# Attention, Fourier mixing and an MLP on one core: the order of every queue planned anew, as the best of 24 plans

## The chip, the cores and the metric

The kernel runs on one core of a Trainium2 chip. The core has a matrix engine (TensorE, PE in the profile), an elementwise engine (VectorE, DVE), an engine for activations (ScalarE, ACT), a general engine (GpSimd, POOL) and a queue engine (SyncE, SP). They run at the same time, each working through its own list of instructions in order, and wait for one another by semaphores. Transfers between DRAM and the on-chip memory run on 16 DMA engines, issued from SP, POOL and ACT. The metric is the device time of one execution in microseconds (us).

## The reference

Inputs are q, k and v of shape 4 × 8 × 768 × 64 (batch, head, position, width), eight memory keys and values for every head, and two weight matrices of 512 × 2048 and 2048 × 512. The computation has two parts:

```python
# attention: chunks of 32 queries see 8 memory keys, 16 keys to the left, the chunk, 8 to the right
scores = scale * np.matmul(q_c, k_full.transpose(0, 1, 3, 2))
a = exp(scores - max); a = a / (sum(a) + 1e-09)
out[:, :, c_start:c_end] = np.matmul(a, v_full)
# x: heads side by side, 4 x 768 x 512
X = np.fft.fft(x, axis=1)
X = np.fft.fft(X, axis=2)
u = x + np.real(X)
un = (u - mu) / np.sqrt(var + 1e-06)
ch = np.maximum(un @ w_ch1, 0.0) @ w_ch2
return (u + ch).astype(np.float32)
```

## The kernel before, in words

**Attention** is done in 16 steps, four for each batch, of two heads each. A step loads q and k (POOL, L345 and L349) and v (SP, L358 to L367, seven transfers) into rings of three and four buffers. For batches 0 to 2, PE turns q and k (L377), ACT copies q and ACT or DVE copies k (L395, L408); batch 3's are turned by transposing transfers on SP (L382, L386). PE makes the scores in two groups (L433), ACT takes the exponential (L441), PE multiplies with the values in two groups (L457, named xa and xo) and DVE normalises into the batch's x (L467, L468).

**Fourier.** The real part of the two-dimensional transform is made by matmuls with tables of sines and cosines. For batches 1 to 3: DVE folds x (L489, L496, L497, L506), ACT rounds to 16 bits (L514), DVE takes the remainder (L519), PE multiplies along the rows of the sequence in four groups of 12 matmuls, one of them with 12 more (L529), ACT rounds (L541), DVE takes the remainder (L546), PE multiplies along the columns (L699) for half of the output tiles and a last row (L580), and DVE adds to x (L705, and L587 with L589 for the mirrored half, which needs a copy of x with its rows in reverse). That copy goes through DRAM: out on POOL (L563), turned by SP (L567 and L568, x_back from x_rows), back on POOL (L572). Batch 0 is done in its own way, so that it can start early: rows in groups L669, L675 and L688, and all six column tiles on PE. DVE then takes statistics (L713, L714), and ACT centres or scales (L720, L724). PE turns batch 0's tiles (L730); SP transposes those of the others (L748).

**MLP**, for each batch in three blocks of two 128-row tiles: 8 first-layer groups (L775) with ReLU on ACT (L784), then the second layer (L793) with the addition on DVE (L800) for batches 0 and 1. For batches 2 and 3 the second layer is made of seven products of half-size blocks (L842); DVE prepares sums and differences of the ReLU's output and of the weights (L830, `e_w2t`), and adds the products (L847).

**What sets the order.** The kernel is not written in its final order. Every piece of work is recorded by `add` as a task: its engine, an estimated cost, the tasks that it comes after, the buffers that it takes and gives back (all named in `Plan(dict(qs=NS, ks=NS, va=NV, ...))`: PSUM banks are tr, sc, xa, two of acc and two of mlp), and a rank. `behind` names a task that must have been placed first on whatever engine, `late` and `lag` shift a time, `moved` is a transfer's size in estimated us. `order` then walks through estimated time and gives each idle engine the lowest-ranked task that can start. The list that it returns is the order in which instructions are emitted, so each engine's queue follows it; the planner's times have no other part in the program. PSUM banks of tasks with `pick` are chosen in that walk too.

```python
for t in plan.order():
    t["emit"]()
```

**Zero products.** While PE has no task to start between the first scores and the first low part of batch 0 (`plan.filling`, which names `t_sc[0, 0]`), the planner places matmuls with zeros (`e_fill`, L902). **The gate.** q and k of step 4 are loaded behind a copy of one element of step 3's v on POOL (`e_gate`, L956), which holds that queue until v has landed. **The weights** are loaded on POOL, the first layer's between steps 5 and 6, the second layer's after step 6 (L1062, L1067).

Of the kernel before, what the change touches and what calls it, by code (L numbers as in the profile page):

```python
# [36 lines left out]
class Plan:  # L37
# [3 lines left out]

    LAG = {"PE": 0.2}
    FIRST = 45.0
    WARM = 18.0
    SLACK = 0.7
    FILL = 0.17
    filling, fill = None, None
# [14 lines left out]
    def share(self, now):  # L62
# [26 lines left out]
        if self.seen < now:  # L89
            self.flow, self.seen = {}, now  # L90

    def order(self):
        now, idle = 0.0, {}
        self.flow, self.seen = {}, 0.0
        waiting, since = {}, {}
# [4 lines left out]
        gives = []  # L100
        placed = []
        while any(waiting.values()):
# [5 lines left out]
            for e, ts_ in waiting.items():  # L108
                if idle.get(e, 0.0) > now:
                    continue  # L110
                held = False
                for t in ts_:
# [28 lines left out]
                    cost = t["cost"] * (2.0 if e == "PE" and now < self.WARM else 1.0)  # L141
                    idle[e] = t["end"] = now + cost
                    if t["moved"]:
                        self.flow.setdefault(e, []).append([t, t["moved"], now + cost * t["head"]])
                        self.share(now)
                        t["end"] = t["done"]
                    else:
# [10 lines left out]
                else:  # L158
                    if e == "PE" and self.filling and self.filling[0]["at"] is not None \
# [5 lines left out]
                        moved = True  # L165
            if not moved:
                times = ([v for v in idle.values() if v > now] + [g[0] for g in gives]
                         + [t["done"] + x for t in placed for x in (0.0, self.SLACK, 4.0, 8.0)
                            if t["done"] + x > now])
# [8 lines left out]
def kernel(  # L178
# [709 lines left out]
    for i in range(NV):  # L888
# [4 lines left out]
                       rank=(0, 1, 2, 3)[i])  # L893
    t_masks = add("POOL", 0.6, e_masks, rank=16)
    dz = cpool.tile([P, P], BF16)
# [42 lines left out]
    t_gate, LATE, t_flip = None, 1.0, [None]  # L938
    t_uz = add("POOL", 0.4, lambda: [nc.gpsimd.memset(kU[i], 0.0) for i in range(NKU)], rank=20)

    def attention(n):
        nonlocal t_gate
        b, pr = seq[n]
        first = b == 0
# [14 lines left out]
        mk = t_mk[n] = add("ACT" if n == HP else "DVE", 0.25, lambda: e_mkT(n), [t_mkT, t_kTz[n % NKT], t_mk.get(n - 1)],  # L959
                           take=("kTb",), behind=t_norm.get((HP - 1, 1)) if n in (HP, HP + 1) else None)  # L960
        if b >= TURNED:
            eq = add("SP", 1.2, lambda: e_flip_q(n), [lq], take=("qT",), give=("qs",),
                     late=5.0, loose=True, behind=t_flip[0])
            t_flip[0] = tk = add("SP", 1.2, lambda: e_flip_k(n), [lk, t_uz], take=("kU",),
                                 give=("ks",), late=5.0, loose=True, behind=eq)
            ek = add("DVE", 0.6, lambda: e_kT(n), [tk, mk], give=("kU",), lag=4.0)
        else:
            tq = add("PE", 0.40, lambda: e_turn_q(n), [lq, t_idb], take=("tr",), give=("qs",))
# [4 lines left out]
            tk = add("PE", 0.43, lambda: e_turn_k(n), [lk, t_idb, t_kz if n == 0 else t_kzs],  # L973
                     take=(ktag,), give=("ks",))
            ek = add(dve[0], 1.25 if dve[1] else 1.04, lambda: e_kT(n, dve[1]), [tk, mk],
                     give=(ktag,))
        xs_ = []
        for g in range(2):
            s_ = add("PE", 0.32, lambda g=g: e_scores(n, g), [eq, ek], take=("sc",),
                     give=("qT", "kTb") if g == 1 else ())  # L980
            t_sc[n, g] = s_
            t_exp[n, g] = x_ = add("ACT", 1.12, lambda g=g: e_exp(n, g),
                     [s_, t_masks, t_after.get(n)], take=("e1",), give=("sc",))
            xs_.append(x_)
            if not first and g == 0:
                continue
            tag = "mlp" if first and g == 1 else "xa"
            if not first:
                vp = dict(of=("mlp", "acc"))
                pick_of["v", n] = vp  # L990
                v_ = add("PE", 1.5, lambda: [e_values(n, i) for i in range(2)],
                         xs_ + [lv, t_low[n % NV]], take=("xa",), pick=vp, give=("e1", "e1", "va"))
                for i in range(2):
# [5 lines left out]
            v_ = add("PE", 0.85, lambda g=g: e_values(n, g), [x_, lv, t_low[n % NV]], take=(tag,),  # L999
                     rank=len(plan.tasks) + (50 if (n, g) == (2, 1) else 25) if first else None,  # L1000
                     give=("e1", "va") if g == 1 else ("e1",))
# [135 lines left out]
    def fourier(b):  # L1137
# [8 lines left out]
        for par in range(2):  # L1146
# [8 lines left out]
            for ab in range(2):  # L1155
# [6 lines left out]
                         give=("fold",) if ab == 1 else ())  # L1162
                rw = add("PE", 1.95 if par == 0 and ab == 1 else 1.0,
                         lambda par=par, ab=ab: e_rows(b, par, ab), [lo, t_sines],
# [4 lines left out]
        return columns_of(b, t_rest)  # L1169

    def columns_of(b, t_rest):
        t_dn, t_un, cols = {}, {}, {}
        allr = list(t_rest.values())
        kts, sa = (0, 1, 2, 3, 4, 5), None
        thirds = set()

# [15 lines left out]
        def columns(kt):  # L1192
            if b > 0 and kt > 2:
                if kt == 3:
                    cols[kt] = add("PE", 0.7, lambda: e_last_row(b), [t_sum[0]])
                return
# [8 lines left out]
        for i, kt in enumerate(kts):  # L1205
# [13 lines left out]
            if b in EVEN:  # L1219
                if i % 2:  # L1220
                    t0, t1 = kts[i - 1], kt
                    sc_ = add("POOL", 2.6, lambda t0=t0, t1=t1: e_scale(b, t0, t1 - t0), [sa])
                    for t in (t0, t1):
                        un = add("ACT", 0.72, lambda t=t: e_un(b, t), [sc_], take=("un",))
# [4 lines left out]
            un = add("ACT", 0.72, lambda kt=kt: e_un(b, kt), [sa], take=("un",))  # L1229
            if b > 0:  # L1230
# [7 lines left out]
                           take=room(kt), give=("mlp",))  # L1238
        return t_un, add("POOL", 1.8, lambda: e_rstd(b), [sa]) if b not in EVEN else None

# [117 lines left out]

    done = {0: first_fourier()}
    for b in range(1, B):  # L1360
# [41 lines left out]
```

## Time and profile before

| | |
|---|---|
| median of three runs | 281.31 us (281.21 to 281.39) |
| profiled execution | 282.55 us |
| its span, first to last instruction | 280.7 us |
| instructions in the span | 7981 |
| first-layer matmuls L775, busy | 90.3 us |
| ReLU L784 on ACT, busy | 56.9 us |
| second-layer matmuls L793, busy | 44.8 us |
| products L842, 128x256, busy | 24.1 us |

"Busy" is the time in which an engine had an instruction running; the shares are of the span. In the list of waits, a line says which instruction of which engine stood still, and which instruction or transfer ended the wait. In a timeline each line is a group of like instructions: its start, its length, engine, line of the program, output and inputs, size, count, and in brackets the idle time ahead of it with what ended it. The page's second part cuts the span into 40 slices; a digit is the busy share in tenths.

The parts of the run: up to about 33 us tables are made and batch 0's attention runs; then PE goes through batch 0's Fourier transform, the MLP of batch 0 with the attention of batches 1 and 2 between, and so on, until from about 220 us only the MLP's blocks of batches 2 and 3 are left.

### The profile page before, as it was taken

The page shows a single profiled execution, that of the slowest core. Times are in us where ns is not written, and L with a number is a line of the kernel's source. Part 1 is how long each engine was busy: PE and PEld are TensorE (multiplying, and loading weights), DVE is VectorE, ACT ScalarE, POOL GpSimd, SP SyncE. Part 2 cuts the span into 40 slices and gives each one's busy share as a digit, 9 for nine tenths or more (in the row PEclk, how much of TensorE's full clock was granted, in tenths as well). Part 3 has the DMA queues.
Part 4 walks back from the last instruction along what each step waited for, and adds up shares of the span by engine and source line. Part 5 has one row for each costly group of instructions (what it writes and reads, how often), then busy time and mean ns, then how long its engine had stood idle before and what let it go on. Part 6 is the DMA issues. An engine that isn't in the chain of part 4 may idle for free.

```text
span 280.7 us, 7981 instructions
## 1 busy us (share of the span) xinstructions
PE 264.3 (94%) x3325; PEld 207.4 (74%) x3325; DVE 193.5 (69%) x424; ACT 155.2 (55%) x262; POOL 64.3 (23%) x127
## 2 busy tenths in 40 slices
PE   0589999999999999998999999999999999999995
PEld 0466698788756579766668766858988888888884
DVE  7968978970218979899688776599869825353444
ACT  6887667579665757734745665525526270605150
POOL 8840853240111038306200230101004100000000
PEclk9999999999999999999999999999999999999999
DMA  6989999999899969999999734497101507103152
GB/s 102 199 143 174 162 206 204 196 198 201 162 190 236 214 103 220 177 142 144 235 191 209 177 74 109 108 207 167 48 37 58 131 21 168 40 37 77 50 103 76
DMA packets 116116, 39.98 MB, mean 142 GB/s; under 512 B 104560, under 2 KB 111472, under 8 KB 116080
## 3 DMA queue, kind: packets, MB, share of 16 engines
q1 hardware_dynamic: 93888, 23.54, 46.9%
q0 software_dynamic: 21472, 15.21, 34.0%
q10 hardware_dynamic: 720, 0.72, 0.7%
q8 instruction: 26, 0.43, 0.7%
q14 instruction: 10, 0.08, 0.1%
HBM read 37.36 MB, written 13.37 MB: 181 GB/s over the span
## 4 chain that ended last, share of the span: by engine, by line
PE 84%; DMA 7%; DVE 4%; SPq 3%; issue 1%; POOL 0%; POOLq 0%
PE ph L775 31%; PE pc L793 15%; PE pc L842 13%; DMA va<-in_v_dram 6%; PE ps L529 6%; PE xa L457 4%; PE pm L699 4%; PE ps L688 3%; PE xo L457 3%; PE sc L433 2%; SPq L358 2%; DMA qs<-in_q_dram 1%; PE trk L377 1%; PE trq L377 1%; DVE xsb L705 1%; PE pm L580 1%
## 5 line engine op out<-in xcount | busy, mean ns | idle before, releaser
L775 PE MATMUL ph<-unT,w_sb 128*128 128x256 f16 x768 | 90.3, 273 | 0.8 <-DVE xsb L800 0.8
L784 ACT ACTIVATE hT<-ph 128x512 f16<-128x512 f32 x96 | 56.9, 598 | 54.3 <-PE pc L842 30.2
L775 PEld LDWEIGHTS <-w_sb 128*128 128x128 f16 x768 | 73.2, 98 | 11.1 <-issue 1.7
L793 PE MATMUL pc<-w_sb,hT 128*128 128x512 f16 x192 | 44.8, 380 | 0.0
L441 ACT ACTIVATE e<-sc,mbias 128x384 f32<-128x384 f32 x64 | 33.6, 576 | 19.0 <-PE sc L433 19.0
L793 PEld LDWEIGHTS <-hT 128*128 128x128 f16 x192 | 17.7, 98 | 19.0 <-issue 0.2
L847 DVE TENSOR_TENSOR xsb<-pc,xsb 128x256 f32<-128x256 f32 x43 | 18.0, 421 | 12.4 <-PE pc L842 10.6
L842 PEld LDWEIGHTS <-hT 128*128 128x128 f16 x240 | 23.3, 98 | 4.2 <-DVE hT L830 1.0
L842 PE MATMUL pc<-w_sb,hT 128*128 128x256 f16 x192 | 24.1, 272 | 0.5 <-DVE hT L830 0.5
L541 ACT CAST up<-ps 128x386 f16<-128x386 f32 x16 | 9.7, 605 | 17.6 <-PE ps L529 17.0
L830 DVE TENSOR_TENSOR S<-hT 128x768 f16<-128x768 f16 (+1 forms) x12 | 5.1, 422 | 18.5 <-ACT hT L784 17.9
L800 DVE SCALAR_TENSOR_TENSOR xsb<-pc,rstd,xsb 128x512 f32<-128x512 f32 x12 | 9.0, 750 | 12.2 <-PE pc L793 12.1
L713 DVE BATCH_NORM_STATS2 st<-xsb 128x6 f32<-128x512 f32 x24 | 16.6, 690 | 0.6
L705 DVE TENSOR_TENSOR xsb<-pm,xsb 128x512 f32<-128x512 f32 x15 | 10.2, 678 | 7.1 <-PE pm L699 6.9
L457 PEld LDWEIGHTS xa<-va,e 128*64 128x64 f32 x384 | 12.5, 137 | 3.2 <-issue 2.0
L457 PE MATMUL xa<-va,e 128*64 128x65 f32 x384 | 14.7, 226 | 0.0
L433 PEld LDWEIGHTS <-kTb 64*128 64x128 bf16 x384 | 7.8, 96 | 9.0 <-issue 8.1
L457 PE MATMUL xo<-va,e 128*64 128x65 f32 x384 | 14.1, 223 | 0.0
L546 DVE TENSOR_TENSOR up<-ps,up 128x386 f16<-128x386 f32 x16 | 9.6, 602 | 6.1 <-ACT up L541 6.1
L395 ACT COPY qT<-trq 128x768 bf16<-128x768 bf16 x12 | 9.5, 793 | 6.4 <-PE trq L377 6.4
L572 POOL DMA_DIRECT2D xr<-x_back x3 | 2.3, 770 | 46.7 <-DMA x_back<-x_rows 46.7
L519 DVE TENSOR_TENSOR lo<-ff,hi 128x768 f16<-128x768 f32 x12 | 11.3, 954 | 2.4 <-ACT hi L514 2.4
(168 smaller groups left out, 455.3 us busy)
## 6 DMA issues: line engine op xcount, KB each, us to landing
va<-in_v_dram SPq DMA_DIRECT2D x32, 220.0 KB
w_sb<-in_moe_w_ch_dram POOLq DMA_DIRECT2D x8, 512.0 KB, 16.9
out_dram<-xsb SPq DMA_DIRECT2D x12, 256.0 KB
qs<-in_q_dram POOLq DMA_DIRECT2D x12, 192.0 KB, 6.5
ks<-in_k_dram POOLq DMA_DIRECT2D x12, 192.0 KB, 7.0
x_rows<-xsb POOLq DMA_DIRECT2D x3, 768.0 KB, 4.6
xr<-x_back POOLq DMA_DIRECT2D x3, 768.0 KB, 5.0
out_rows<-xsb SPq DMA_DIRECT2D x9, 256.0 KB
```

The source lines that it names most:

```text
L433: nc.tensor.matmul(sc[:, hh, t6, :], kT[r0:r0 + 64, t, :], qT[r0:r0 + 64, ts(t, 64)], start=True, stop=True, tile_position=(r0, 0))
L441: nc.scalar.activation(e1[:, :, :, ts(half, 32)], sc[:, :, 0:6, ts(half, 32)], AFT.Exp, bias=mbias[:, half:half + 1], scale=1.0 / math.sqr ...
L457: nc.tensor.matmul(xa[64 * half:64 * half + 64, st, hh, 0:65], e1[:, hh, t6, :], v1[:, hh, 6 * g + t6, 0:65], start=True, stop=True)
L519: nc.vector.tensor_tensor(lo[:, ab].rearrange(fl), ff_of[b, par][:, ab].rearrange(fl), hi[:, ab].rearrange(fl), ALU.subtract)
L529: nc.tensor.matmul(out_[:, sp, :], part[:, ab, sp * 3 + st, c0:c1], tab[:, sp, st, :], start=(st == 0 and i == 0), stop=(st == 2 and i == 1))
L705: nc.vector.tensor_tensor(uv, pm_of[b, kt], uv, ALU.add)
L713: nc.vector.bn_stats(st6, xs[b][:, kt, :])
L775: nc.tensor.matmul(ph[:, k, :], w1_sb[:, dt, ts(HH * k + i, P)], unT_of[b, j][:, dt, :], start=(dt == 0), stop=(dt == NDT - 1))
L784: nc.scalar.activation(hT_of[b, j][:, :, i, :], ph, AFT.Relu, bias=0.0, scale=1.0 if b in EVEN else -1.0)
L793: nc.tensor.matmul(pc_of[b, j, r], hT_of[b, j][:, k, i, ts(r, P)], w2_sb[:, HH * k + i, :], start=(i + k == 0), stop=(i + k == HH))
L842: nc.tensor.matmul(pc_of[key], a[:, i, :], w[:, i, :], start=(i == 0 and new), stop=(i == HH - 1), skip_group_check=not new)
L847: nc.vector.tensor_tensor(u, pc, u, ALU.add)
```

## The change

The planner is changed, some estimated costs, and what some tasks wait for. No instruction is computed otherwise than before.

- `shortest(24, 1.5)` takes the place of `order()`. It runs the walk 24 times, once with the ranks as they are and 23 times with a random draw of spread 1.5 added to each rank (not for batch 0's tasks, those before `lead`, and not for ranks over 1e5), and then takes the plan with the earliest estimated end.
- The walk frees DVE and ACT a little before a task's result is ready (`OVER`), and holds SP's queue while a large transfer has more than 2.2 us to go (`full`, `ROOM`).
- Estimated costs are set anew: masks 0.6 to 0.86, the zeroing of kU 0.4 to 1.5, loads of q and k 0.9 to 0.66, turns 0.40 to 0.46 and 0.43 to 0.48, scores 0.32 to 0.30, exponentials 1.12 to 1.05, rows 1.0 to 1.02 and 1.95 to 2.2, and others.
- Uses of the same buffer in the rings (qs, ks, va, kTb, kU) are written down as dependencies (`t_used`), the second group of scores is placed behind the first, and values behind the values before.
- The loads of v of steps 14 and 15 are placed behind `t_x2[2]`, the turn of batch 2's rows; before, they were behind `t_x2[1]`.

In the program that results, 22 zero products are emitted instead of 29, each queue's order is another, and nothing else differs.

```diff
+    def shortest(self, tries, spread):
+
+        free, ranks = dict(self.free), [t["rank"] for t in self.tasks]
+        found = None
+        for i in list(range(tries)) + [None]:
+            draw = random.Random(found[1] if i is None else i)
+            even = (found[1] if i is None else i) == 0
+            self.free = dict(free)
+            for t, rank in zip(self.tasks, ranks):
+                move = draw.gauss(0.0, spread)
+                t["rank"] = rank if even or rank < self.lead or rank > 1e5 else rank + move
+                t["done"] = t["at"] = None
+                if t["pick"] is not None:
+                    t["pick"].pop("tag", None)
+            placed = self.order()
+            if found is None or self.end < found[0]:
+                found = (self.end, i)
+        return placed
...
-                if idle.get(e, 0.0) > now:
+                if idle.get(e, 0.0) > now or (e == "SP" and self.full and self.full["done"] - self.ROOM > now):
...
-                    idle[e] = t["end"] = now + cost
+                    idle[e] = t["end"] = now + cost - (0.0 if t["moved"] else self.OVER.get(e, 0.0))
...
-        lq, lk = [add("POOL", 1.6 if b >= TURNED else 0.9, lambda i=i: e_load_qk(n, i),
+        lq, lk = [add("POOL", 1.66 if b >= TURNED else 0.66, lambda i=i: e_load_qk(n, i), [t_used.get((i, at))],
...
-        lv = add("SP", 2.5, lambda: e_load_v(n), [t_ones[n] if n < NV else None],
+        lv = add("SP", 2.5, lambda: e_load_v(n), [t_ones[n] if n < NV else None, t_used.get(("va", n % NV))],
...
+        t_used[0, at], t_used[1, at] = (eq, tk) if b >= TURNED else (tq, tk)
...
-            s_ = add("PE", 0.32, lambda g=g: e_scores(n, g), [eq, ek], take=("sc",),
-                     give=("qT", "kTb") if g == 1 else ())
+            s_ = add("PE", 0.30, lambda g=g: e_scores(n, g), [eq, ek], take=("sc",),
+                     give=("qT", "kTb") if g == 1 else (),
+                     behind=t_sc.get((n, 0)))
...
+    t_lv[14]["behind"] = t_x2[TURNED - 1]
+    t_lv[15]["behind"] = t_x2[TURNED - 1]
+
     with tc.manual_schedule():
-        for t in plan.order():
+        for t in plan.shortest(24, 1.5):
             t["emit"]()
```

More of the change, by code (lines that the diff above doesn't have):

```diff
@@ L1 @@
 import math
+import random
 from contextlib import ExitStack
@@ L42 @@
     LAG = {"PE": 0.2}
+    OVER = {"DVE": 0.08, "ACT": 0.1}
     FIRST = 45.0
@@ L45 @@
     SLACK = 0.7
+    lead = 0
+    ROOM = 2.2
     FILL = 0.17
@@ L90, in share @@
             self.flow, self.seen = {}, now
+    def shortest(self, tries, spread):
[15 more added lines that the diff above has]
+        return placed
     def order(self):
         now, idle = 0.0, {}
-        self.flow, self.seen = {}, 0.0
+        self.flow, self.seen, self.full = {}, 0.0, None
         waiting, since = {}, {}
@@ L100, in order @@
         gives = []
-        placed = []
+        placed, recent, known = [], [], 0
         while any(waiting.values()):
@@ L146, in order @@
                         t["end"] = t["done"]
+                        if e == "SP" and t["moved"] > 2.5:
+                            self.full = t
                     else:
@@ L166, in order @@
             if not moved:
+                recent = [t for t in recent if t["done"] + 8.0 > now] + placed[known:]
+                known = len(placed)
                 times = ([v for v in idle.values() if v > now] + [g[0] for g in gives]
-                         + [t["done"] + x for t in placed for x in (0.0, self.SLACK, 4.0, 8.0)
+                         + ([self.full["done"] - self.ROOM] if self.full else [])
+                         + [t["done"] + x for t in recent for x in (0.0, self.SLACK, 4.0, 8.0)
                             if t["done"] + x > now])
@@ L893 @@
                        rank=(0, 1, 2, 3)[i])
-    t_masks = add("POOL", 0.6, e_masks, rank=16)
+    t_masks = add("POOL", 0.86, e_masks, rank=16)
     dz = cpool.tile([P, P], BF16)
@@ L938 @@
     t_gate, LATE, t_flip = None, 1.0, [None]
-    t_uz = add("POOL", 0.4, lambda: [nc.gpsimd.memset(kU[i], 0.0) for i in range(NKU)], rank=20)
+    t_uz = add("POOL", 1.5, lambda: [nc.gpsimd.memset(kU[i], 0.0) for i in range(NKU)], rank=20)
+    t_used = {}
     def attention(n):
@@ L943, in attention @@
         b, pr = seq[n]
+        at = n % NS
         first = b == 0
-        lq, lk = [add("POOL", 1.6 if b >= TURNED else 0.9, lambda i=i: e_load_qk(n, i),
+        lq, lk = [add("POOL", 1.66 if b >= TURNED else 0.66, lambda i=i: e_load_qk(n, i), [t_used.get((i, at))],
                       take=(("qs", "ks")[i],), moved=3.1 if b >= TURNED else 1.2, grain=0.032 if b >= TURNED else 0.1, late=LATE if b else 2.0,
@@ L958, in attention @@
             t_gate = add("POOL", 0.1, e_gate, [lv])
-        mk = t_mk[n] = add("ACT" if n == HP else "DVE", 0.25, lambda: e_mkT(n), [t_mkT, t_kTz[n % NKT], t_mk.get(n - 1)],
+        mk = t_mk[n] = add("ACT" if n == HP else "DVE", 0.25, lambda: e_mkT(n), [t_mkT, t_kTz[n % NKT], t_mk.get(n - 1), t_used.get(("kTb", n % NKT))],
                            take=("kTb",), behind=t_norm.get((HP - 1, 1)) if n in (HP, HP + 1) else None)
@@ L963, in attention @@
                      late=5.0, loose=True, behind=t_flip[0])
-            t_flip[0] = tk = add("SP", 1.2, lambda: e_flip_k(n), [lk, t_uz], take=("kU",),
+            t_flip[0] = tk = add("SP", 1.2, lambda: e_flip_k(n), [lk, t_uz, t_used.get(("kU", n % NKU))], take=("kU",),
                                  give=("ks",), late=5.0, loose=True, behind=eq)
             ek = add("DVE", 0.6, lambda: e_kT(n), [tk, mk], give=("kU",), lag=4.0)
+            t_used["kU", n % NKU] = ek
         else:
-            tq = add("PE", 0.40, lambda: e_turn_q(n), [lq, t_idb], take=("tr",), give=("qs",))
+            tq = add("PE", 0.46, lambda: e_turn_q(n), [lq, t_idb], take=("tr",), give=("qs",))
             dve = ("DVE", nc.vector.tensor_copy) if n < HP else ("ACT", None)
@@ L972, in attention @@
             ktag = "acc" if first else "tr"
-            tk = add("PE", 0.43, lambda: e_turn_k(n), [lk, t_idb, t_kz if n == 0 else t_kzs],
+            tk = add("PE", 0.48, lambda: e_turn_k(n), [lk, t_idb, t_kz if n == 0 else t_kzs],
                      take=(ktag,), give=("ks",))
@@ L976, in attention @@
                      give=(ktag,))
+        t_used[0, at], t_used[1, at] = (eq, tk) if b >= TURNED else (tq, tk)
         xs_ = []
         for g in range(2):
-            s_ = add("PE", 0.32, lambda g=g: e_scores(n, g), [eq, ek], take=("sc",),
-                     give=("qT", "kTb") if g == 1 else ())
+            s_ = add("PE", 0.30, lambda g=g: e_scores(n, g), [eq, ek], take=("sc",),
+                     give=("qT", "kTb") if g == 1 else (),
+                     behind=t_sc.get((n, 0)))
+            t_used["kTb", n % NKT] = s_
             t_sc[n, g] = s_
-            t_exp[n, g] = x_ = add("ACT", 1.12, lambda g=g: e_exp(n, g),
+            t_exp[n, g] = x_ = add("ACT", 1.05, lambda g=g: e_exp(n, g),
                      [s_, t_masks, t_after.get(n)], take=("e1",), give=("sc",))
@@ L992, in attention @@
                          xs_ + [lv, t_low[n % NV]], take=("xa",), pick=vp, give=("e1", "e1", "va"))
+                t_used["va", n % NV] = t_used["v", n] = v_
                 for i in range(2):
@@ L1000, in attention @@
                      rank=len(plan.tasks) + (50 if (n, g) == (2, 1) else 25) if first else None,
-                     give=("e1", "va") if g == 1 else ("e1",))
+                     give=("e1", "va") if g == 1 else ("e1",),
+                     behind=t_used.get(("v", n)))
+            t_used["va", n % NV] = t_used["v", n] = v_
             take = ("xsb",) if g == 0 and n % HP == 0 else ()
@@ L1162, in fourier @@
                          give=("fold",) if ab == 1 else ())
-                rw = add("PE", 1.95 if par == 0 and ab == 1 else 1.0,
+                rw = add("PE", 2.2 if par == 0 and ab == 1 else 1.02,
                          lambda par=par, ab=ab: e_rows(b, par, ab), [lo, t_sines],
@@ L1169, in fourier @@
         return columns_of(b, t_rest)
+    t_flips = {}
     def columns_of(b, t_rest):
@@ L1174, in columns_of @@
         kts, sa = (0, 1, 2, 3, 4, 5), None
+        t_flips[b] = t_un
         thirds = set()
@@ L1194, in columns @@
                 if kt == 3:
-                    cols[kt] = add("PE", 0.7, lambda: e_last_row(b), [t_sum[0]])
+                    cols[kt] = add("PE", 0.75, lambda: e_last_row(b), [t_sum[0]])
                 return
@@ L1221, in columns_of @@
                     t0, t1 = kts[i - 1], kt
-                    sc_ = add("POOL", 2.6, lambda t0=t0, t1=t1: e_scale(b, t0, t1 - t0), [sa])
+                    sc_ = add("POOL", 1.7, lambda t0=t0, t1=t1: e_scale(b, t0, t1 - t0), [sa])
                     for t in (t0, t1):
-                        un = add("ACT", 0.72, lambda t=t: e_un(b, t), [sc_], take=("un",))
+                        un = add("ACT", 0.78, lambda t=t: e_un(b, t), [sc_], take=("un",))
                         t_un[t] = add("SP", 1.2, lambda t=t: e_flip(b, t), [un],
@@ L1228, in columns_of @@
                 continue
-            un = add("ACT", 0.72, lambda kt=kt: e_un(b, kt), [sa], take=("un",))
+            un = add("ACT", 0.78, lambda kt=kt: e_un(b, kt), [sa], take=("un",))
             if b > 0:
@@ L1238, in columns_of @@
                            take=room(kt), give=("mlp",))
-        return t_un, add("POOL", 1.8, lambda: e_rstd(b), [sa]) if b not in EVEN else None
+        return t_un, add("POOL", 2.05, lambda: e_rstd(b), [sa]) if b not in EVEN else None
     mlp_prev, t_sums, side_end = [None], [], []
@@ L1359 @@
     done = {0: first_fourier()}
+    plan.lead = len(plan.tasks)
     for b in range(1, B):
```

## The prediction

> **What bounds the kernel now.** I read the page's busy list and slices first, then TensorE's waits, then the timeline around each wait that the new order touches.
>
> ```profile
> span 280.7 us, 7981 instructions
> ...
> PE 264.3 (94%) x3325; PEld 207.4 (74%) x3325; DVE 193.5 (69%) x424; ACT 155.2 (55%) x262; POOL 64.3 (23%) x127
> ...
> PE   0589999999999999998999999999999999999995
> ...
> DVE  7968978970218979899688776599869825353444
> ```
>
> One digit is 7.02 us. TensorE (PE) is full from the fourth slice to the last, so the end is PE's start, its dense work, its holes, and a tail. VectorE (DVE) stands at 8 and 9 over long stretches: it is the next bound there. What PE waited for, in us in total, times, longest:
>
> ```profile
> PE mps L1015 <- DVE mkb L1009: 7.2, 1, 7.2
> PE trq L377 <- DMA qs<-in_q_dram: 2.1, 3, 1.4
> ...
> PE ph L775 <- DVE xsb L800: 0.8, 1, 0.8
> PE pm L699 <- DVE xsb L705: 0.7, 2, 0.5
> PE pc L842 <- DVE hT L830: 0.5, 2, 0.2
> ```
>
> The first is the start, before there is data; most of the second is a DMA at 12 us. An order of the same work can win little more than the other three and what lies around them.
>
> ```profile
> 30.90 0.92 PE L457 MATMUL xo<-va,e 128*64 128x65 f32 x24
> 32.21 0.53 PE L377 MATMUL trq<-ident_b,qs 96*64 96x96 bf16 x16 [0.39 <-DMA qs<-in_q_dram]
> 32.67 0.66 PE L902 MATMUL idle<-dz 128*128 128x384 bf16 x3
> 33.17 0.33 PE L669 MATMUL ps<-dz 128*128 128x386 bf16 x1
> ```
>
> Step 4's turn of q waits for a load (issued at 27.98, landed at about 32.2) whose queue was held by the one-element copy at L956 until v of step 3 was in. Three zero products follow, then batch 0's Fourier rows begin at 33.17. From there to PE's last group at 277.52 is 244.35 us. Summing each group by its own row gives 240.2 us of dense work with 38 changes of group kind (0.1 us each) among it. Holes that I can place add up to about 3.2 us: 0.9 among batch 0's columns (47 to 55), 0.98 at 127, 1.36 at the five places where product 3 follows product 6 (0.41 twice, 0.18 three times); the remaining 0.9 us is scatter of single groups.
>
> **The change part by part.** The instructions are the same but for 7 of 29 zero products; all else is their order on each queue. I laid PE's new order beside the old, gave each group its duration in the trace (8 first-layer matmuls 0.87 us, 4 second-layer 0.86, columns 0.87, rows 1.01, or 2.21 with the extra row, a values pair 1.55, scores 0.28, turns 0.46 and 0.48), and looked where an input is late. Dense work: 240.1 us with 37 changes, so −0.1.
>
> *Start.* Five of the seven removed products (0.165 to 0.19 us each) stood before step 3's last values, which so end about 0.95 us sooner. But step 4's turn still waits for its load, and the first twelve v loads on SP, the copy at L956 and the loads ahead of it on POOL keep their order. The 0.95 us become a longer wait, about 0.8 instead of 0.39, with the three products that now stand ahead of the turn. Behind the turn one product stands where three did: 2 × 0.165 less, the rows begin at 32.86. I take −0.31. Bounds: −0.95 if the load too came as much earlier, which nothing in its chain suggests; +0.2 if it lands later.
>
> *Batch 0's columns.* The order of before put two scores and step 4's k turn among the Fourier rows; the new one runs them densely and has only that turn (0.48) between the last rows and the first columns. How long the hand-over takes:
>
> ```profile
> 45.27 0.61 ACT L541 CAST up<-ps 128x386 f16<-128x386 f32 x1
> ...
> 45.91 0.61 DVE L546 TENSOR_TENSOR up<-ps,up 128x386 f16<-128x386 f32 x1 [0.20 <-ACT up L541]
> ```
>
> The last rows ended at 45.16 and the remainder at 46.52, 1.36 us. Less 0.48 leaves a hole of 0.9, where before the turn of q and both values covered it. The later waits on the column sums shrink, since turns and scores now stand between the columns: 1.34 for the stage instead of 0.90, +0.44. Bounds 0 and +1.0 (nothing else shrinks).
>
> *The hole at 127.* Batch 0's last second-layer group ended at 127.9; batch 1's first group wanted the very bank that it had filled, so it waited for DVE's addition (L800, 128.09 to 128.84) and began at 128.87. In the new order batch 1's column banks are read by 119.5 and the values' bank by 121.8, before that point (126.5), so another bank is free and this hole goes. What is late next: batch 1's five scalings on ACT (L720, 0.72 each in the trace) now stand between the ReLUs of batch 0's last block, which hold PE's banks; two in a row put a ReLU 1.44 us back, and 1.1 us of matmuls in two free banks cover that. I take a hole of 0.35 (0.2 to 1.1) for the 0.98: −0.63, between −0.8 and +0.1.
>
> *Batch 2 moved up.* Its rows start at position 130.0 instead of 138.0, its columns at 145.0 instead of 155.1. The chain of before, on DVE:
>
> ```profile
> 127.02 0.56 DVE L468 TENSOR_TENSOR xsb<-xo,zs 128x384 f32<-128x384 f32 x1
> ...
> 128.76 0.95 DVE L489 TENSOR_TENSOR zy<-xsb 128x768 f32<-128x768 f32 x1
> ...
> 135.65 0.96 DVE L519 TENSOR_TENSOR lo<-ff,hi 128x768 f16<-128x768 f32 x1 [1.74 <-ACT hi L514]
> ```
>
> From the last normalisation's start to the low part is 9.6 us. I walked DVE's new queue from batch 1's columns (at 110.3 and 111.1): four sums, two mirrored sums, six statistics (0.69 to 0.87 each) bring it to 120.3, the normalisations to 121.8, folds, two additions and one weight sum to the first low part at 129.4. PE wants it at 130.0: 0.4 us to spare after the release. The second pair of rows (138.4) has 0.1 to 0.3. So this costs between 0 and 0.65 as walked; I take +0.4, since spare times this thin do not all hold.
>
> *Batch 2's second block of products* now has column groups and the last row between products 6 and 3, so DVE's subtraction is covered: −0.41 (0 if they fall elsewhere). The four other places stay.
>
> *The last two v loads* now go behind the turn of batch 2's rows on SP (766 KB in small pieces). SP's queue holds step 12's and 13's transposes ahead of it as before; behind it wait v of steps 14 and 15, batch 2's flips and steps 14 and 15's transposes. Values 14 and 15 stand at 173.6 and 184.6, over 30 us after that turn: their cover is 30 us of second-layer work, so 0; without cover it would be the 7 us that a v load takes at the start. Batch 3's rows move from 188.7 to 196.6, their first-layer groups from 236.8 to 233.2, with some 2 us in hand for the last flips: 0, up to +1 if SP is late. From batch 2's last products on both orders are the same, and so is the tail (277.52 to 280.7).
>
> Sum: −0.10 −0.31 +0.44 −0.63 +0.40 −0.41 = −0.61 us.
>
> [...] Turns of 16 took 0.85 us until 14.6 and 0.53 from 17.9 on, and no wait of PE after the first turn was longer than 1.39 us. [...]
>
> **The rivals.** *A, holes filled better than I walk* (−1.8, 279.5): batch 0's columns are no worse than before, the hole at 127 goes whole, batch 2 is in time: −0.10 −0.31 −0.98 −0.41. For it: 1.36 us is little to cover. Against it: the turn of 0.48 is all that stands there.
> *B, no change* (+0.3, 281.6): the start gives nothing (load 0.3 later), and the ReLU wait is as long as the old hole: −0.10 +0.44 +0.40 −0.41 = +0.33. For it: a start set by the same load; ACT was 64% busy from 100 to 120. Against it: both would have to lie at their far bounds.
> *C, slower* (+0.9, 282.2): DVE is late with batch 2. If its chain takes 10.5 us from the first normalisation to the end of the low part, as in before (126.13 to 136.61), instead of the 9.1 that I walk, the rows stall 1.0 us, and the second pair 0.9 again: the sum without its +0.40 is −1.01, plus 1.9. It turns slower when DVE is over 0.9 us late in each. For it: 8.6 to 8.9 us busy of 10 there, 8 us less time. Against it: the 10.5 held 3 us of waits for PE and ACT.
>
> **How the numbers follow.** Forecast 40%, A 15%, B 17%, C 28%. The profiled execution took 282.55 us, 1.85 more than its span and 1.24 above the median of the runs (281.31), so I put the sum against it (281.94) and take the same difference from the median: 280.7. The forecast's own range is 280.1 to 281.4, from the bounds of columns and ReLU. Over all: 279.6 leaves out half of A, 282.6 the worse third of C. Under 0.2% (0.56 us) this measurement hardly tells a change from none: of the forecast 24 of 40 lie below 280.75, so faster is 0.24 + 0.15 = 0.39 and some of B's near side, 0.41; same the rest of the forecast and most of B, 0.28; slower C and the far end of B, 0.31.
>
> **What would show it.** In the changed profile: 22 zero products; the turn of step 4 at 32.2 after a wait of 0.8 on its load, rows at 32.9; a wait of the first columns on DVE L546 near 44 to 45; no wait on L800 near 127, but one of L775 on ACT L784 near 117; rows of batch 2 near 130 waiting under 0.5 us; four waits at L842 instead of five. Wrong: a wait on L519 or L546 over 1 us between 128 and 150, first-layer groups of batch 3 waiting for SP's flips, or PE's last group not between 276.5 and 277.5.

## The result

The changed kernel takes 280.75 us (median of 13 executions, 280.26 to 281.81) against 282.04 for the kernel before beside it: ratio 0.9958, 95% interval 0.9938 to 0.9978, so 0.2 to 0.6% faster. Single executions of the kernel before scatter in this series from 281.2 to 287.3 us, those of the changed one within 1.6 us, so the median of before, and every ratio to it, depends on which are drawn (medians of 282.6 to 282.8 in later series); part of what follows is why. In the later series 18 of 88 executions of before, 283.7 to 285.7 us long, had a mean granted TensorE clock of 0.994, where the others and all 25 of the changed kernel have 0.998 to 1.0; by an estimate (0.006 of 284 us) the clock is 1.7 us of what they are longer, and no such execution was profiled.

The changed kernel's page, its size and the slices of PE and DVE (line numbers are 28 to 38 higher than before: L775 is now L803, L842 is L870, L705 is L733, L546 is L574, L748 is L776):

```profile
span 279.2 us, 7959 instructions
...
PE 264.8 (95%) x3318; PEld 208.3 (75%) x3318; DVE 192.6 (69%) x424; ACT 154.7 (55%) x262; POOL 63.5 (23%) x127
...
PE   0599999999999999999999999999999999999995
...
DVE  7968999941238999999937851259987975353444
```

The span is 1.5 us shorter. The work is the same; PE's digits of 8 in slices 3 and 19 have become 9s. What PE waits for now (us in total, times, longest):

```profile
PE sc L461 <- POOL va L345: 0.9, 1, 0.9
PE trq L405 <- ACT qT L423: 0.8, 1, 0.8
PE pc L870 <- DVE xsb L875: 0.6, 2, 0.4
PE trq L405 <- DMA qs<-in_q_dram: 0.5, 1, 0.5
PE ph L803 <- ACT hT L812: 0.2, 1, 0.2
```

The waits of first-layer groups and columns on DVE (L800 and L705 before) are gone. The wait of a product on DVE is another one, and a first-layer group waits for ACT, as the prediction had it. The timeline of PE at the start of batch 0's rows:

```profile
30.25 0.92 PE L485 MATMUL xo<-va,e 128*64 128x65 f32 x24
31.10 0.66 PE L930 MATMUL idle<-dz 128*128 128x384 bf16 x3
31.69 0.53 PE L405 MATMUL trq<-ident_b,qs 96*64 96x96 bf16 x16
32.16 0.34 PE L930 MATMUL idle<-dz 128*128 128x384 bf16 x1
32.33 0.33 PE L697 MATMUL ps<-dz 128*128 128x386 bf16 x1
```

The rows begin at 32.33 instead of 33.17, and step 4's turn did not wait for its load at all.

For all kernels below I took PE's groups in their order, and from the start of each to the start of the next took off the group's usual duration (the ones that the prediction lists). What is left over are the holes:

| kernel | rows start | holes behind it | PE's last group starts | median us | planner's estimate of the end |
|---|---|---|---|---|---|
| before | 33.17 | 3.98 | 276.48 | 282.04 | 276.24 |
| before, second profile | 32.85 | 4.34 | 276.52 | 282.6 | 276.24 |
| changed | 32.33 | 3.40 | 274.95 | 280.75 | 274.81 |
| changed, second profile | 33.27 | 3.30 | 275.80 | 280.57 | 274.81 |
| old order, two v loads late | 32.17 | 3.01 | 274.51 | 280.77 | |
| changed, two v loads early | 32.28 | 4.58 | 276.09 | 281.78 | |
| changed, one plan | 32.23 | 4.00 | 275.56 | 281.58 | 276.07 |
| old planner, best of 24 | 32.39 | 3.99 | 275.51 | 281.83 | 276.16 |
| changed, worst of 24 | 31.70 | 5.02 | 275.95 | 282.35 | 277.20 |
| changed, best of 96 | 32.33 | 2.23 | 273.77 | 279.75 | 273.73 |

Between the first and the third line: −0.84 in the rows' start, −0.58 in the holes, −0.1 in changes of group kind: −1.53 us in all. Between the second profiles of the two kernels it is +0.42, −1.04 and −0.1, −0.72 us in all: the holes shrink both times, the start goes either way.

### The profile page after: what moved, and what is told of

Same layout as the page of the kernel before. It is cut to its first block, busy times and chain, and to the rows that moved or that the text cites. A ratio compares the mean times of both kernels' runs of the same rounds, so it can differ in the third digit from the quotient of the medians.

```text
span 279.2 us, 7959 instructions
## 1 busy us (share of the span) xinstructions
PE 264.8 (95%) x3318; PEld 208.3 (75%) x3318; DVE 192.6 (69%) x424; ACT 154.7 (55%) x262; POOL 63.5 (23%) x127
## 4 chain that ended last, share of the span: by engine, by line
PE 82%; DVE 6%; POOL 5%; DMA 2%; ACT 2%; issue 2%; POOLq 0%; DVEq 0%
PE ph L803 26%; PE pc L821 15%; PE pc L870 11%; PE ps L557 6%; PE pm L727 5%; PE xa L485 4%; PE xo L485 4%; PE ps L716 3%; PE sc L461 3%; DMA qs<-in_q_dram 2%; PE trq L405 2%; PE trk L405 1%; PE idle L930 1%; ACT un L752 1%; PE pm L608 1%
## 5 line engine op out<-in xcount | busy, mean ns | idle before, releaser
L803 PE MATMUL ph<-unT,w_sb 128*128 128x256 f16 x768 | 90.0, 273 | 0.2 <-ACT hT L812 0.2
L803 PEld LDWEIGHTS <-w_sb 128*128 128x128 f16 x768 | 73.6, 98 | 10.8 <-issue 0.8
L469 ACT ACTIVATE e<-sc,mbias 128x384 f32<-128x384 f32 x64 | 33.6, 580 | 17.7 <-PE sc L461 17.7
L870 PEld LDWEIGHTS <-hT 128*128 128x128 f16 x240 | 23.3, 98 | 3.9 <-issue 1.0
L870 PE MATMUL pc<-w_sb,hT 128*128 128x256 f16 x192 | 24.1, 273 | 0.2 <-DVE xsb L875 0.2
L858 DVE TENSOR_TENSOR S<-hT 128x768 f16<-128x768 f16 (+1 forms) x12 | 5.1, 424 | 16.4 <-ACT hT L812 15.8
L485 PEld LDWEIGHTS xa<-va,e 128*64 128x64 f32 x384 | 13.1, 143 | 3.6 <-issue 2.9
L485 PE MATMUL xa<-va,e 128*64 128x65 f32 x384 | 15.4, 232 | 0.0
L752 ACT ACTIVATE un<-xsb,rs 128x512 f16<-128x512 f32 x12 | 9.5, 807 | 10.1 <-POOL rs L767 10.1
L485 PEld LDWEIGHTS xo<-va,e 128*64 128x64 f32 x384 | 13.0, 142 | 0.4 <-ACT ff L651 0.3
L542 ACT CAST hi<-ff 128x768 f16<-128x768 f32 x12 | 9.9, 830 | 4.9 <-DVE ff L534 4.7
L461 PE MATMUL sc<-qT,kTb 64*128 64x64 bf16 x384 | 11.6, 196 | 0.9 <-POOL va L345 0.9
L870 PE MATMUL pc<-w_t,S 128*128 128x256 f16 x96 | 11.6, 272 | 0.4 <-DVE xsb L875 0.4
```

Source lines behind the costliest of these rows:

```text
L461: nc.tensor.matmul(sc[:, hh, t6, :], kT[r0:r0 + 64, t, :], qT[r0:r0 + 64, ts(t, 64)], start=True, stop=True, tile_position=(r0, 0))
L469: nc.scalar.activation(e1[:, :, :, ts(half, 32)], sc[:, :, 0:6, ts(half, 32)], AFT.Exp, bias=mbias[:, half:half + 1], scale=1.0 / math.sqr ...
L485: nc.tensor.matmul(xa[64 * half:64 * half + 64, st, hh, 0:65], e1[:, hh, t6, :], v1[:, hh, 6 * g + t6, 0:65], start=True, stop=True)
L752: nc.scalar.activation(un, xs[b][:, kt, :], AFT.Identity, bias=rs[:, 1:2], scale=rs[:, 0:1])
L803: nc.tensor.matmul(ph[:, k, :], w1_sb[:, dt, ts(HH * k + i, P)], unT_of[b, j][:, dt, :], start=(dt == 0), stop=(dt == NDT - 1))
L870: nc.tensor.matmul(pc_of[key], a[:, i, :], w[:, i, :], start=(i == 0 and new), stop=(i == HH - 1), skip_group_check=not new)
```

## The experiments

**The same kernel before, profiled again.** No edit.

> The kernel before, once more, for a second profile of its start. In its first profile the copy at L956 ran at 27.44 and the rows began at 33.17; in the profile of the changed kernel the copy ran at 25.70 and the rows began at 32.33, though SP and POOL have the same instructions ahead of it. If the loads' timing differs from execution to execution, this profile shows a copy somewhere between 25.5 and 27.5 and rows 0.5 us earlier than in the first where the copy is early. If the order is the cause, it shows 27.4 and 33.2 again. The hole at L800 near 127 (0.98) and the ones at L842 (0.41 twice, 0.18 three times) should be the same to 0.1 us.

The copy at L956 ran at 25.78, the turn of step 4 did not wait, the rows began at 32.85. The hole near 127 had grown from 0.98 to 1.35, and its releaser was another than in the first profile. The timeline of PE and, below it, SP's queue, in this second profile:

```profile
123.68 4.05 PE L793 MATMUL pc<-w_sb,hT 128*128 128x512 f16 x18
128.91 0.82 PE L775 MATMUL ph<-unT,w_sb 128*128 128x256 f16 x6 [1.18 <-DMA unT<-un]
```

```profile
119.96 1.33 SPq L382 DMA_TRANSPOSE qT<-qs  x1
121.40 3.84 SPq L748 DMA_TRANSPOSE unT<-un  x3
125.35 1.23 SPq L386 DMA_TRANSPOSE kU<-ks  x1
```

Batch 1's first layer waited for the transposes of its own input. In the first profile the wait had been put down to DVE's addition (L800), which happened to end at the same moment: the trace of that profile has the landing of the last transpose that PE's weight loads waited for at 128.73, the addition's end at 128.84. The prediction built on that reading. The three transposes are issued at 121.4 (in the first profile at 123.7), and ahead of them in SP's queue stands the load of v of step 14. Its seven transfers hold the queue from 112.18 to 119.79 (to 121.22 in the first profile), with 1.7 us (2.9) of waits for v transfers issued earlier and one issue of 2.34 us (3.34):

```profile
112.18 0.59 SPq L362 DMA_DIRECT2D va<-in_v_dram  x1
113.44 1.53 SPq L358 DMA_DIRECT2D va<-in_v_dram  x2
115.03 1.00 SPq L367 DMA_DIRECT2D va<-in_mem_v_dram  x1
116.15 3.28 SPq L358 DMA_DIRECT2D va<-in_v_dram  x2
119.48 0.31 SPq L367 DMA_DIRECT2D va<-in_mem_v_dram  x1
```

So a new theory: not the choice among plans, but the two lines that put v of steps 14 and 15 behind the turn of batch 2's rows make the gain, by clearing SP's queue for the transposes. The rival: the choice of a plan makes it, and the two loads matter little. These were told apart from both sides.

**The old order with the two loads late.** The list of the planner of before, with two entries moved:

```diff
-        for t in plan.order():
+        placed = plan.order()
+        for n in (15, 14):
+            placed.remove(t_lv[n])
+            placed.insert(1 + [t is t_x2[2] for t in placed].index(True), t_lv[n])
+        for t in placed:
             t["emit"]()
```

> The kernel before, order and all, with only the loads of v of steps 14 and 15 moved behind the turn of batch 2's rows on SP. If they held up the flips, the hole near 127 (0.98 and 1.35 in two profiles) goes, and with it the tail of slow executions (up to 285 to 287 us): about 1.0 us less than before, 280.8 to 281.5, most of the gain of the whole change. If not, the hole stays and the median stays at 281.5 to 282.8.

280.77 us (280.55 to 281.41) where before had 282.6 in the same series: ratio 0.9951 (0.9933 to 0.9970). The whole change had 0.9953 (0.9933 to 0.9974), 280.57 us, in that series. The three transposes of batch 1 are issued earlier, and the hole near 127 is gone: in SP's queue and on PE

```profile
118.06 4.52 SPq L748 DMA_TRANSPOSE unT<-un  x3
122.69 1.23 SPq L386 DMA_TRANSPOSE kU<-ks  x1
```

```profile
120.85 6.21 PE L793 MATMUL pc<-w_sb,hT 128*128 128x512 f16 x28
126.89 2.35 PE L775 MATMUL ph<-unT,w_sb 128*128 128x256 f16 x20
```

the first layer follows the second without a gap. It begins at 126.89, before the last addition L800 (DVE), while PE's order and its banks are those of before; so the bank was not what held it there:

```profile
127.09 0.75 DVE L800 SCALAR_TENSOR_TENSOR xsb<-pc,rstd,xsb 128x512 f32<-128x512 f32 x1 [0.52 <-PE pc L793]
```

Every other hole is the one of before to 0.02 us. Two loads moved in an otherwise untouched order give what the whole change gives, and the long tail of single executions goes with them.

**The changed order with the two loads early.** The other way round: only v of step 14 goes back ahead of batch 1's first transposes, v of step 15 ahead of its last.

```diff
+        for n, ahead in ((14, [t_used["v", 10], t_lv[13]]), (15, [t_used["v", 11], t_flips[1][2]])):
+            placed.remove(t_lv[n])
+            at = max(i for i, t in enumerate(placed) if any(t is x for x in ahead))
+            placed.insert(at + 1, t_lv[n])
```

> The changed kernel's order, with only the loads of v of steps 14 and 15 put back to where the old order had them on SP: 14 ahead of batch 1's first flips, 15 ahead of the last. If those loads held up the flips in the old order, the hole where batch 1's first layer begins (126 to 129) comes back, 0.5 to 1.4 us by a wait on unT from a DMA: 281.3 to 282.2, and the times scatter more, as they do before. If that hole came from a bank or from DVE, nothing changes: within 0.2 us of the changed kernel.

281.78 us, 1.2 more than the changed kernel beside it (280.57), and the scatter is back (280.7 to 285.2). But the hole is not where I expected it: the first layer at 126 found its input. In this order v of step 14 is through SP's queue at 113.7, and batch 1's first transposes are issued at 114.60, only 0.7 us later than in the changed kernel. The hole, 1.24 us, opened at 142, by way of DVE (timeline of DVE and PE):

```profile
142.28 0.43 DVE L443 COPY kTb<-kU 128x1056 bf16<-128x1056 bf16 x1 [3.26 <-DMA kU<-ks]
142.63 0.58 DVE L574 TENSOR_TENSOR up<-ps,up 128x386 f16<-128x386 f32 x1
```

```profile
143.26 0.24 PE L557 MATMUL ps<-sinS,hi 128*128 128x193 f16 x1 [1.08 <-DVE up L574]
```

The last two k transposes on SP were late by the loads ahead of them (issued at 131.61 and 136.30, in the changed kernel at 123.88 and 129.71); DVE's queue stood 3.26 us on the copy of a transposed k, with the remainder of batch 2's rows behind it, and PE waited 1.1 us for the bank that this frees. The cause is of the same kind, a transpose behind a v load, but the place is another.

**The changed planner with one plan.** All of the change but the choice of 24.

```diff
-        for t in plan.shortest(24, 1.5):
+        for t in plan.shortest(1, 1.5):
```

> The changed planner with its costs and ties, but one plan with the ranks as they are, instead of the best of 24. If the gain of the change comes from the choice among plans, nearly all of it goes: ratio to the kernel before 0.998 to 1.002. If it comes from the corrected costs and the ties, the ratio stays near 0.996. By the planner's own estimates this plan ends 1.26 us after the chosen one (276.07 against 274.81) and 0.17 before the old plan (276.24).

281.58 us (281.12 to 282.22, and one execution of 309.5): 0.8 to 1.0 more than the changed kernel, measured in another series. The ratio to before in its own series, 0.9943 (0.9915 to 0.9971), lies where the expectation had it for a gain by costs and ties, so between choice and costs the two measures do not agree. By holes it loses 0.6 to 0.7, at 118 (0.62, ReLU) and 196 to 199 (1.06 in three pieces, DVE's additions). Neither theory was whole: the two lines are in this kernel too, and it has no hole at 127, but the new costs and ties (the uses of one buffer written down as dependencies) with ranks as they are make a plan that is worse elsewhere than the old one: 4.00 us of holes, where before has 3.0 without the one at 127. The choice wins that back. Costs and ties were not run apart from each other.

**The old planner with the best of 24.** Only `shortest` and `lead` added to the kernel before.

> The planner of before, its costs, its waits and no ties, with only the choice of the best of 24 random plans added. If choosing is enough by itself, it gains like the change: ratio 0.996. If the ties are what makes plans usable, nothing is gained: the best of these 24 is estimated at 276.16, 0.08 earlier than the old plan, the others up to 285; ratio 0.999 to 1.005, slower where the loose order makes an engine wait for a buffer that the estimate did not see.

281.83 us, ratio 0.9960 (0.9928 to 0.9991). It should have gained nothing by its own estimate (276.16 against 276.24), and did gain: its draw happened to lose the hole at 127, and found one of 0.95 near 166. In SP's queue of this draw v of step 14 stands behind the first three transposes of batch 1 (these from 117.25, the load from 124.72), so this run speaks for the loads once more, not for choosing as such; the scatter is gone here too (281.31 to 282.60). The old estimates of the 24 plans run up to 285, the new ones only from 274.8 to 277.2: the costs or the ties keep the draws together.

**The worst of the 24.**

```diff
-            if found is None or self.end < found[0]:
+            if found is None or self.end > found[0]:
```

> The changed planner with the worst of its 24 plans instead of the best: estimated 2.4 us later (277.20 against 274.81). If the estimates rank plans as the chip does, this is 1.5 to 2.5 us slower than the changed kernel, ratio to before 1.001 to 1.005. If the ranking is mostly noise on the chip, it is within 0.5 us of the changed kernel: ratio 0.995 to 0.998.

282.35 us, 1.6 to 1.8 after the changed kernel, 2.4 by the estimates; the ratio to before, 0.9969 (0.9939 to 0.9999), is below what was expected, as the median of before was 282.79 in this series. With the other plans of the new planner (last column of the table) the estimates rank four plans as the chip does: 273.73, 274.81, 276.07, 277.20 became 279.75, 280.6 to 280.75, 281.58, 282.35, in three series.

**The best of 96.**

```diff
-        for t in plan.shortest(24, 1.5):
+        for t in plan.shortest(96, 1.5):
```

> The changed kernel with the best of 96 plans instead of 24; the planner estimates its end at 273.73, 1.08 us before the chosen one of 24 (274.81). If the estimates rank plans (worst, at 277.20, came 1.6 to 1.8 us after the changed kernel, one plan, at 276.07, 0.8 to 1.0): 279.6 to 280.1. If holes that the estimate does not see decide (0.4 to 0.6 each in all plans so far), 280.2 to 281.2.

279.75 us (six executions, 279.19 to 280.13): ratio to before 0.9886 (0.9843 to 0.9928). The hole at 117 is gone and the one at 196 is 0.17. No other version is faster.

**Two instructions moved by hand.** On DVE one low part behind one addition, on ACT one scaling behind one ReLU.

```diff
+        for t, ahead in ((t_low_part[3, 0, 0], t_sum_up[2, 0, 1, 0]), (t_center[1, 4], t_relu[0, 2][4])):
+            placed.remove(t)
+            placed.insert(1 + [x is ahead for x in placed].index(True), t)
```

> The changed kernel's order with two instructions each put one place later: on DVE batch 3's first low part (L547) behind the first addition of batch 2's first products (L875), for the hole of 0.58 near 196; on ACT batch 1's fourth scaling (L748) behind the fifth ReLU, for the hole of 0.39 near 117. If holes of TensorE go into the time one for one, both go and the median is 0.9 to 1.0 us less than the changed kernel's 280.57: 279.6 to 279.8. If another wait takes their place (the low part 0.4 later for the rows, the flip 0.6 later), 280.0 to 280.6.

280.34 us (279.86 to 280.75), 0.2 to 0.4 less than the changed kernel. The hole that they were for, in the changed kernel (DVE, then PE):

```profile
195.89 0.95 DVE L547 TENSOR_TENSOR lo<-ff,hi 128x768 f16<-128x768 f32 x1
196.76 1.27 DVE L875 TENSOR_TENSOR xsb<-pc,xsb 128x256 f32<-128x256 f32 x3
```

```profile
197.23 1.03 PE L870 MATMUL pc<-w_t,S 128*128 128x256 f16 x8 [0.41 <-DVE xsb L875]
```

The product waits for an addition that stands behind a low part. Swapped, this hole of 0.58 went, but one of 0.34 came at 201, where the rows now wait for the remainder that DVE reaches later; and the hole of 0.39 by the ReLU became one of 0.20. Half of the holes came back elsewhere: sum 3.3 to 3.4 before, 2.89 after.

**More zero products in the idle stretches of the start.** The clock of PE was cold longer with the new start in the first profiles (a turn of 16 still took 0.88 at 18.3, where before it was 0.53 at 17.9). Two kernels add zero products where PE has nothing to do; `early_zeros` has 21, 4 and 4 of them, `kept_warm`:

```diff
+        on_pe = [t for t in placed if t["engine"] == "PE"]
+        for ahead, more in ((0, 37), (3, 8), (4, 7)):
+            at = 1 + [t is on_pe[ahead] for t in placed].index(True)
+            placed[at:at] = [dict(engine="PE", emit=plan.fill)] * more
```

> The changed kernel once more, as the measure for the next three on the same chip: 280.5 to 281.2 us. Its profile shows again no wait for flips near 127, a hole of about 0.4 near 117 and of about 0.6 near 196, and the rows' start between 31.7 and 32.4. If its clock warms again only by 18 to 20 us, as in the three profiles with this start, the fewer zero products before 16 us are the likelier cause; if by 16.5, it was chance.

> The changed kernel with 29 more zero products where PE stands idle at the start anyway: 21 ahead of the first transpose (1.4 to 8 us) and 4 in each of the two waits at 10.5 and 12. If the clock follows what PE has done lately, it is warm by 9 us, the cold turns, scores and values of 9 to 20 us take about half (3 us of PE time), and the chain of scores and exponentials begins earlier: rows 0.3 to 1.0 us earlier, 279.6 to 280.6. If loads and ACT hold that stretch, the durations shrink and the rows start as before: within 0.2 us of the changed kernel. If the 8 products in the waits run cold, they delay the first scores by 0.5 to 1 us and the start is later.

> The changed kernel with 52 more zero products: 37 ahead of the first transpose, so that PE is busy up to about 8.7 us, and 8 and 7 in the two waits at 10 and 12 us. With 21, 4 and 4 the clock was full at 9, then half from about 10.5 to 21 us, after a wait of 2.7 us and two shorter ones. If idle stretches took it down, it now stays full from 9 on: turns 0.53, values 0.92 from the start, and the rows begin 0.3 to 1.0 us earlier if no load is late: 279.6 to 280.4. If the clock falls all the same, the 15 products in the waits run at half speed, delay the first scores by up to 2.5 us, and the rows start later: 280.6 to 282.

The second profile of the changed kernel was cold until 18.5, but so was the old order with late loads until 19, with 29 zero products: the order alone does not decide when the clock comes up. It may have a part: three of four profiles of the old start were fast by 16.4, and none of seven of the new one before 17.7 (`one_plan` first: scores of 12 in 0.35 us at 17.75, where they took 0.50 at 15.91). Its rows began at 33.27, with a wait of 1.2 on q's load. `early_zeros` (280.20) and `kept_warm` (280.24, with one of ten executions at 286.44) differ in what the clock did. Turns in `early_zeros`, then in `kept_warm`:

```profile
8.94 0.53 PE L405 MATMUL trq<-ident_b,qs 96*64 96x96 bf16 x16
11.28 0.85 PE L405 MATMUL trq<-ident_b,qs 96*64 96x96 bf16 x16 [0.70 <-ACT qT L423]
18.71 0.88 PE L405 MATMUL trk<-turn_b,ks 100*64 100x100 bf16 x16
```

```profile
11.99 0.53 PE L405 MATMUL trq<-ident_b,qs 96*64 96x96 bf16 x16
17.36 0.55 PE L405 MATMUL trk<-turn_b,ks 100*64 100x100 bf16 x16
```

The windows of `early_zeros` (stretch, its length, busy time with instructions of PE, PEld, DVE, ACT and POOL, then the granted clock, the DMA share and GB/s):

```profile
9.00:10.00 1.00, 1.00 (x35) 0.87 (x35) 0.93 (x3) 1.00 (x3) 0.96 (x2) 1.00 1.23 198
10.00:13.00 3.00, 2.30 (x23) 1.35 (x22) 2.93 (x8) 2.98 (x5) 2.50 (x10) 0.59 1.30 207
13.00:17.00 4.00, 4.00 (x64) 2.46 (x64) 3.19 (x13) 2.63 (x6) 3.44 (x12) 0.50 0.98 181
17.00:21.00 4.00, 4.00 (x77) 3.63 (x76) 2.25 (x5) 3.95 (x6) 0.83 (x2) 0.53 1.04 179
21.00:25.00 4.00, 4.00 (x110) 3.03 (x108) 3.20 (x10) 3.28 (x5) 0.00 (x0) 1.00 0.83 153
```

With 21 products PE was idle from 6.1 to 8.8; the granted clock was full at 9 and then about half until 21. With 37 it had no such gap and stayed fast: turns of 16 took 0.52 to 0.55 us from 9.77 to 30.95, with a granted clock of 1.00 from 5 to 25. The rows then began at 31.58, the earliest of all profiles (the worst plan has 31.70), and loads and ACT kept the rest. Both medians are 0.3 to 0.4 below the changed kernel's, with ranges that overlap its: a small gain is likely, not shown.

**Both together.** The best of 96 plans with the products of `kept_warm`.

> Both changes that gained by themselves: the best of 96 plans (279.75) and the 52 zero products that keep the clock up in the idle stretches of the start (280.24, against 280.57 for the changed kernel). Rows at 31.4 to 31.9 instead of 32.3, then the holes of the plan of 96. If the two add up, 279.2 to 279.6; if loads late in the start eat the second, 279.6 to 280.0.

279.82 us, no less than the plan of 96 alone. The clock stayed up (turns of 16 in 0.52 to 0.55 us from 8.98 on), but q's load for step 3 came late (1.28 us of wait at 22.6) and the rows began at 32.47: in this profile the start was held by a load. Whether a quicker PE brings that on or chance does is open, since the changed kernel's second profile, with a cold clock, has a wait as long (1.24).

## Why the prediction was right, and where it was not

The forecast of −0.61 us (280.7) met a median of 280.75; the direction and the range held. That 280.7 fits so well is luck: the forecast started from 281.31, the median of three executions at the low end of the scatter of before, and beside 282.04 the change is −1.29 us, twice the forecast. One of its own signs of being wrong came about, too: PE's last group ended at 275.99, outside 276.5 to 277.5 (at 276.84 in the second profile). By steps, it was right for partly wrong reasons.

- *Dense work* (−0.1): what is left of −1.53 behind start and holes is −0.11.
- *Start* (−0.31): in the two profiles shown −0.84, but the start scatters with the loads. The old start order gave 33.17, 32.85, 32.39 and 32.17, the new one 32.33, 33.27, 32.23, 31.70, 32.28 and 32.31: means 32.65 and 32.35, so −0.3. The means fit, but with a scatter of 1.0 and 1.6 us they do not show that the start moved at all. The sentence that step 4's turn still waits for its load was wrong: it did not in the changed kernel's first profile, and three of four profiles of the old order show no such wait either; the values ahead of the turn set it.
- *Batch 0's columns* (+0.44): wrong. The hole behind the last rows is 0.17, not 0.9, and the stage's holes fell from 0.9 to about 0.5. The hand-over time was right (about 1.3 us); what was missed is that a column group reads the four row blocks one after another:

```profile
43.64 0.66 PEld L727 LDWEIGHTS <-up 128*128 128x128 f16 x7
...
43.91 0.60 DVE L574 TENSOR_TENSOR up<-ps,up 128x386 f16<-128x386 f32 x1
...
44.56 0.88 PEld L727 LDWEIGHTS <-up 128*128 128x128 f16 x9 [0.26 <-DVE up L574]
```

  Seven of the first group's eight weight loads (PEld) run before the last remainder is there, and cover most of the wait for it.
- *The hole at 127* (0.98 gone, 0.35 in its place): both numbers held (0.98 to 1.35 gone, 0.40 by a ReLU at 117), and so did the cause of the second: with one scaling moved behind a ReLU it fell to 0.20. The cause of the first did not, and its number is luck. It was no bank but the transposes on SP, held up by a v load. The step that failed is the reading of one wait line in one profile.
- *Batch 2 moved up* (+0.40): nothing. The rows began at 130.55 without a wait; the low parts were done at 129.6 and 130.5, as walked. Rival C, DVE late there, did not come about in this order; with late transposes (v loads early) it did, at 142. (Its sum has a slip: −1.01 plus twice 0.5 is already nothing, so it would have turned slower well before DVE was 0.9 us late in each pair.)
- *The second block of products* (−0.41): right. Not in the sum was the first block: +0.58 where its product waits for an addition behind a low part, so five such places are left and not four.
- *The last two v loads* (0, up to +1): the step that failed most. I asked whether the loads would be late for their readers, 30 us ahead, and not what stood behind them in SP's queue before: the transposes of batch 1's input. Moved alone, they are worth the whole change (280.77 us against 280.57), and they end the scatter of the kernel before.
- *Fewer zero products and the clock* (not in the sum): PE's waits behind 20 us stayed under 1.3 us, and the turn right behind the longest of them (1.28 us, in `wide_warm`) took 0.53 us. In `early_zeros` the clock fell, to 0.50 and 0.53 between 13 and 21 us, behind a gap of 2.7 us and one of 0.7.

What remains open: how much of the start's −0.3 is the fewer zero products, since the loads move it by up to 1.6 us from one profile to the next; and what the new costs and the ties are worth without the two loads.

## What to carry to other kernels

When a transfer is moved in a queue, price first what it stops holding up, and only then whether it comes late itself; transposes that feed the next stage should not stand behind a load that is slow to issue (in the second profile of before, v of step 14 held SP's queue for 7.6 us, from 112.18 to 119.79, and the hole that followed was 1.35 us). A wait that one profile puts down to an engine may belong to a DMA that ended at the same moment (128.84 and 128.73 in the first profile of before): look at a second profile, and at the scatter of the times, before building on it. Where the estimates rank plans as the chip does, as for four plans here, trying more of them is cheap: 96 plans instead of 24 gave another 0.8 to 1.0 us, where moving two instructions by hand gave 0.2 to 0.4.

## What the runs showed of the hardware

The old start order came to full clock at 16.4 us in three profiles (values of 24 matmuls in 0.92 us) and at about 19 in a fourth (1.57 us at 16.4), after 3 to 6 us of dense matmuls (PE busy 2.00 us of 2 in 13 to 15 and in 15 to 17 in all four). In `early_zeros` a gap of 2.7 us on PE, with one of 0.7 soon after, was followed by half speed from about 10.5 to 21 us, through 8 us of dense work (granted clock 0.50 and 0.53). In the profiles without added zero products the same column reads 1.00 while a turn of 16 takes 0.85 instead of 0.53 us, so there only the durations tell it. The way back was longer in `early_zeros` (8 us of dense work) than in the four profiles of the old start order (3 to 6 us).

The landing of v and q in the first 30 us varied by over 2 us between profiles of kernels with the same instructions ahead of it (the copy behind v of step 3 at 25.15 to 27.44).
